# Tile 7's first matrix product: fifteen products per 3x3x2 group, in PSUM chains, in place of seven per 2x2x2 group

## The chip, the cores and the metric

The kernel runs on one core of one Trainium2 chip. The metric is the device time of one execution in microseconds (us), the median of several runs; lower is better. The profile is of one further execution, taken by the hardware profiler.

## The reference

An attention block (RWKV6) is followed by a two-layer block with an exact GELU:

```python
# r, k, v, w: (4, 8, 768, 48), u: (8, 48)
for t in range(S):
    cur = einsum('bhd,bhe->bhde', u * k[t], v[t])
    y[t] = einsum('bhd,bhde->bhe', r[t], state + cur)
    state = w[t][..., None] * state + einsum('bhd,bhe->bhde', k[t], v[t])
x = y.transpose(0, 2, 1, 3).reshape(3072, 384)
h = x @ w_in                       # (384, 2048)
g = 0.5 * h * (1 + erf(h / sqrt(2)))
out = g @ w_out                    # (2048, 384)
```

Everything is float32.

## The kernel before

The 3072 tokens are eight tiles of `T` = 384 tokens. For tile x, `attention(x)` leaves the transposed result in `xT` (three blocks of 128 features by 384 tokens), and `mlp(x)` computes `h` in blocks of 128 columns of `w_in` (16 blocks), the gelu `g` and the output `o`. Both are Python generators. In stage x, a string `PLAN[x]` says in which order they issue: each `.` is the next step of `mlp(x - 1)`, each `s` the next step of `attention(x)`, `f` of `attention(x + 1)`, `l` a load, `x` a sum of parts of `xT` that the next h needs, `w` a step of weight preparation. What the string has not used up is issued at the end of the stage, and after the last stage `mlp(7)` runs alone. Every engine executes its own instructions in the order of issue; waits between engines follow from the data.

In stage 7 the 45 `.` are tile 6's h (27 steps) and its o (18), the 34 `s` the rest of `attention(7)`. Of that, TensorE has the products `kv_ps` (L727), `y_ps` (L768, inside a chunk) and the second part of `y_ps` (L813, from the states); VectorE computes the states `st` from `kv_ps` in a sequential chain (L742) and then reads one column of each `y_ps` (L780, called `fence`). `kv_ps` and `y_ps` come from one pool of two pairs of PSUM banks, so a `y_ps` takes over the banks of a `kv_ps`. ScalarE copies `y_ps` to `xT` (L836, L839), and six small transfers on the SP queue (L843) move the last features of a head to their place.

For tiles 2 to 7, h comes from `h_halves` (L949). Of the three feature blocks, two are taken with the two halves of the weight columns and the two halves of the tokens as a 2x2x2 product by seven products (Winograd's form), the third is multiplied plainly. Per pair of blocks (four pairs `q`) the steps are `first` to `seventh`; every call of `two` issues two matmuls of 192 columns for each factor, by `multiply` (L945). Partial sums go by ScalarE copies (L988, L981, L1008, L1012) and VectorE adds (L999, L1017), the gelu is L977. `h_sums` (L886) has replaced `w_in`'s first feature block in the second half of the columns by a sum with the second, in place, and `sums_of_x` (L907) makes five sums of parts of `xT` (L913). A last part, `rest`, is issued in the middle of the first output product.

`o` comes from `product` (L1082; L1084 is the matmul): eight products of 192 columns each, seven times for two thirds of the tile, and again seven-product forms for the last thirds of two tiles together. `of_g` (L931) makes three sums of parts of `g` for it on VectorE (L937, L939, L941). L1132, L1138, L1141, L1144, L1153, L1181 are VectorE's steps between the output products, `psum()` gives them the banks `mm` (two, shared with `h_ps`).

TensorE issues a float32 product as two instructions, and the counts in the profile are of instructions.

Of the kernel before, what the change touches and what calls it, by code (L numbers as in the profile page):

```python
# [10 lines left out]
F32 = mybir.dt.float32  # L11
# [6 lines left out]
AF = mybir.ActivationFunctionType  # L18
ALU = mybir.AluOpType
PSUM = bass.MemoryType.PSUM  # L20

C = 64
G = 64
D = 48
T = 384
# [7 lines left out]
BANK = 512  # L33
# [28 lines left out]
        "sss.sls.....s......ls.s....s.sssssss..s.....s.ss....s.s.ssss.s.l.ss.l.ls.l...s.l.lslssf.s."  # L62
        ".ffs..lff.xx..xffxffx"
    ),
    7: "......s.s....s.s...s.ssssss...sss.ss...sss..ssss.s...ss...s...s.s.ss.s.s.s.x.x...xxx",
}


def as_float(bits):
# [4 lines left out]
def kernel(  # L74
# [25 lines left out]
    nc = tc.nc  # L100
    NX = rkw.shape[0]
# [4 lines left out]
    NJ = DM // 128  # L106
# [9 lines left out]
    gp = ctx.enter_context(tc.tile_pool(name="gp", bufs=4))  # L116
# [3 lines left out]
    pools = {"d": pairs_of_banks.enter_context(tc.tile_pool(name="pd", bufs=3, space=PSUM))}  # L120
# [3 lines left out]

    def fewer_pairs():
        pairs_of_banks.close()
        pools["d"] = ctx.enter_context(tc.tile_pool(name="pe", bufs=2, space=PSUM))
        pools["u"] = ctx.enter_context(tc.tile_pool(name="pu", bufs=1, space=PSUM))
        for i in range(2):
            u = bank_u(i)  # L130
            nc.tensor.matmul(u, lhsT=zeros[:, 0:128], rhs=zeros, start=True, stop=True)

    def bank_u(i):
        return pools["u"].tile([128, BANK], F32, name="u_ps", tag=f"u{i % 2}")

    def bank(name="o_ps"):
        return ps.tile([128, BANK], F32, name=name, tag="mm", bufs=2)
# [11 lines left out]
    bufs = [io.tile([128, 3 * NP * T], F32, name=f"rkw{i}", bufs=1) for i in range(2)]  # L149
    ALL = NP * T  # L150
# [48 lines left out]
    WI = PIECE // NJ  # L199
    FP = PIECE // DM  # L200
    FI = WI // 128
    w_in_sb = const.tile([128, DF // WI, NJ, WI], F32, name="w_in_sb")
    ins = [(w_in_sb[:, i], w_in.rearrange("(j p) (i c) -> p i j c", p=128, c=WI)[:, i]) for i in range(DF // WI)]
    outs = [(w_out_sb[:, f:f + FP, :], w_out.rearrange("(f p) c -> p f c", p=128)[:, f:f + FP, :]) for f in range(0, NF, FP)]
    pieces = ins + outs
# [50 lines left out]
    for h in masks:  # L256
        if not h:
# [5 lines left out]
                                op0=ALU.logical_shift_right, op1=ALU.logical_shift_left)  # L263
# [4 lines left out]
    a_sb = const.tile([128, 2, NPART * NI, C], F32, name="a_sb")  # L268
# [7 lines left out]
    kx = const.tile([128, 2 * NPART * NI * 3 * C // 2], F32, name="kx")  # L276
# [7 lines left out]
    for i, h in enumerate(QUARTERS[:1]):  # L284
        for a in range(3):
            w_q = (3 - a) * C // 4
            z = q_ints[1 if a == 0 else 2]
            o = i * C if a < 2 else i * C + C // 2
# [18 lines left out]
    def make_quarter_masks():  # L307
        make_fine()
        yield
        for (h, a), m_q in m_qs.items():  # L310
            nc.vector.tensor_tensor(out=quarter[h][a], in0=s_qs[h][:, 0:m_q.shape[1]], in1=m_q, op=ALU.is_equal)
            yield
# [5 lines left out]
    s_home = const.tile([128, DF // 2], F32, name="s_home")  # L318
# [48 lines left out]
    xT_of = {}  # L367
# [480 lines left out]
    FG = 4  # L848
    sums, s3_sb = [], []

    def w_quarter(b, c, k):
        return w_out_sb[:, b * HF + k * FG:b * HF + (k + 1) * FG, c * HM:(c + 1) * HM]

    def w_sums():

        sums.extend(cv.tile([128, HF, HM], F32, name="t", tag="raw", bufs=AHEAD) for _ in range(3))
        for out_, x, y in ((0, (0, 1), (0, 0)), (1, (1, 1), (0, 1)), (0, (1, 1), 0), (2, (1, 0), 0)):
            for k in range(2):
                o = sums[out_][:, k * FG:(k + 1) * FG]
                nc.vector.tensor_sub(o, w_quarter(*x, k), sums[y][:, k * FG:(k + 1) * FG] if isinstance(y, int) else w_quarter(*y, k))  # L860
                yield

    def first_sum():
        for k in range(2):
            nc.vector.tensor_sub(w_quarter(0, 1, k), w_quarter(0, 1, k), w_quarter(0, 0, k))
            yield


    HT = T // 2
    HK = HF // 2  # L870
    s_of, x_sums, s12_of = [], [], {}

    def homes():

        more = [cv.tile([128, PIECE], I64, name="s", tag="raw", bufs=AHEAD).bitcast(F32) for _ in range(2)]
        s3_sb.append(more[0][:, 0:HF * 128].rearrange("p (f c) -> p f c", f=HF))
        x_sums.extend(z[:, i * HT:(i + 1) * HT] for z in (more[0][:, HF * 128:], more[1][:, HF * 128:]) for i in range(2))
        spare = [cv.tile([128, PIECE], F32, name=name) for name in ("f", "f", "e", "e")]
        for i, name in enumerate(("s1", "s2")):
            s12_of[name] = [z[:, 0:FG * 128].rearrange("p (f c) -> p f c", f=FG) for z in spare[2 * i:2 * i + 2]]  # L880
        second = [more[1][:, i * WI:(i + 1) * WI] for i in range(HK)]
        third = [s_home[:, i * WI:(i + 1) * WI] for i in range(HK)]
        fourth = [z[:, FG * 128:] for z in spare]
        s_of.extend((second, third, fourth))

    def h_sums():  # L886

        def w(a, c, k):
            return w_in_sb[:, a * HK + k * 2:a * HK + k * 2 + 2, c, :]

        def pieces_of(i, k):
            return s_of[i - 2][2 * k:2 * k + 2]

        for k in range(2):
            for i in range(2):
                nc.vector.tensor_sub(pieces_of(3, k)[i], w(0, 0, k)[:, i], w(1, 0, k)[:, i])
            yield
            nc.vector.tensor_add(w(1, 0, k), w(1, 0, k), w(1, 1, k))
            yield
            for i in range(2):  # L900
                nc.vector.tensor_sub(pieces_of(2, k)[i], w(1, 0, k)[:, i], w(0, 0, k)[:, i])
            yield
            for i in range(2):
                nc.vector.tensor_sub(pieces_of(4, k)[i], w(0, 1, k)[:, i], pieces_of(2, k)[i])
            yield

    def sums_of_x(x):  # L907

        xT = xT_of[x]
        x00, x01, x10, x11, l0, l1 = (xT[:, c, b * HT:(b + 1) * HT] for c in range(3) for b in range(2))  # L910
        t2, t3, t4, l01 = x_sums
        for o, a, b in ((t3, x11, x01), (x01, x01, x00), (t2, x11, x01), (t4, x10, t2), (l01, l0, l1)):
            nc.vector.tensor_sub(o, a, b)  # L913
            yield

    def mlp(x):
# [3 lines left out]
        xT = xT_of.pop(x)  # L920
        halves = x > 0
        waits, ends = x % 2 == 0, x % 2 == 1
        gs = {}
# [25 lines left out]
        def h_halves():  # L949
# [108 lines left out]
                gelu(q, 1, 1, g_of(q, 1, 1))  # L1058
            late[:] = [rest]

        s1, s2, s3 = [], [], []
        fast = x > 1
        if fast:
            yield from h_halves()
        for n, group in enumerate(() if fast else (0, 2, 1, 3) if halves else range(4)):
            gs[group] = gp.tile([128, FG, T], F32, name="g")
            for f in range(group * FG, (group + 1) * FG):
                h_ps = bank("h_ps")[:, 0:T]
                for j in range(NJ):
                    nc.tensor.matmul(h_ps, lhsT=w_in_sb[:, f // FI, j, f % FI * 128:(f % FI + 1) * 128], rhs=xT[:, j, :],  # L1070
                                     start=(j == 0), stop=(j == NJ - 1))
                t = T - 128 if waits else T
# [31 lines left out]
        def psum():  # L1104
            return bank()[:, 0:HM]
# [6 lines left out]
        if halves:  # L1112
            o_sb = two_rows()
            p1, u2, u3 = (wk.tile([128, HM], F32, name=name, bufs=1) for name in ("p1", "u2", "u3"))
# [27 lines left out]
            for c in range(2):  # L1142
                z = o_sb[1][:, c * HM:(c + 1) * HM]
# [16 lines left out]
        else:  # L1160
            o_ps = [bank()[:, 0:DM] for _ in range(2)]
            for f in range(NF):
                for i, o in enumerate(o_ps):
                    nc.tensor.matmul(o, lhsT=block(i, f // HF, f % HF), rhs=w_out_sb[:, f, :],  # L1164
                                     start=(f == 0), stop=(f == NF - 1))
# [8 lines left out]
        if waits:  # L1174
            _, o2, o1 = psum(), psum(), psum()
# [8 lines left out]
        elif ends:  # L1184
            o_sb = two_rows()
            p1, u2, u3 = p1_alone, *(wk.tile([128, HM], F32, name=name, bufs=1) for name in ("u2", "u3"))
# [14 lines left out]
            for c in range(2):  # L1201
                z = o_sb[1][:, c * HM:(c + 1) * HM]
# [19 lines left out]
    def next_v():  # L1222
        load_v(1, nc.sync)
        yield

    def warm():
        for _ in range(2):
            keep_warm(3, True)
            yield

    def masks_and_sums():
        yield from make_quarter_masks()
        yield from w_sums()
# [3 lines left out]
    for x in range(NX):  # L1237
        if x == 2:
            homes()
        following = attention(x + 1, 0) if x + 1 < NX else iter(())  # L1240
        if x == 0:
            streams = {
                ".": units[0], "s": units[1], "f": following, "c": pieces_of_w, "w": next_v(), "x": warm(),
                "l": chain(weight_in(0, True), islice(second, 5), weight_in(1, True), second, weight_in(2, True)),
            }
        else:
            streams = {
                ".": mlp(x - 1), "s": slots, "f": following,
                "l": load(x + 1, nc.sync),
                "x": sums_of_x(x) if x > 1 else iter(()),  # L1250
                "w": masks_and_sums() if x == 1 else chain(first_sum(), h_sums()) if x == 2 else iter(()),
                "c": pieces_of_w if x == 1 else iter(()),
            }
        for c in PLAN[x]:
            next(streams[c], None)
        for c in ".slxw" if x == 0 else ".slxwc":
            while next(streams[c], streams) is not streams:
                pass
        slots = following
        if x == 1:  # L1260
            fewer_pairs()
    for _ in mlp(NX - 1):
        pass
# [60 lines left out]
```

## Time and profile before

| | us |
|---|---|
| median of 3 runs | 593.41 (592.35 to 593.92) |
| span of the profiled execution, first to last instruction | 595.0 |
| time around that span | none is given |
| TensorE busy, weight loads busy | 576.7, 512.3 |
| VectorE, ScalarE, GpSimdE busy | 440.0, 281.3, 8.0 |
| granted TensorE clock, mean | 0.994 |

In the profile's lines PE is TensorE, PEld its weight loads, DVE VectorE, ACT ScalarE, POOL GpSimdE, SP the queue of DMA issues; `L945` is line 945 of the kernel. A line of the timeline has the start, the length, the engine, the line, the operation, what is written and read, and in brackets how long the engine stood before it and what ended that. The matmuls of L945 start 0.1625 us apart and are shown with 0.326 us each, so they overlap. The profiled execution took 1.6 us more than the median of the runs, so differences are carried over, not times.

### The profile page before, as it was taken

The page shows a single profiled execution, that of the slowest core. Times are in us where ns is not written, and L with a number is a line of the kernel's source. Part 1 is how long each engine was busy: PE and PEld are TensorE (multiplying, and loading weights), DVE is VectorE, ACT ScalarE, POOL GpSimd, SP SyncE. Part 2 cuts the span into 40 slices and gives each one's busy share as a digit, 9 for nine tenths or more (in the row PEclk, how much of TensorE's full clock was granted, in tenths as well). Part 3 has the DMA queues.
Part 4 walks back from the last instruction along what each step waited for, and adds up shares of the span by engine and source line. Part 5 has one row for each costly group of instructions (what it writes and reads, how often), then busy time and mean ns, then how long its engine had stood idle before and what let it go on. Part 6 is the DMA issues. An engine that isn't in the chain of part 4 may idle for free.

```text
span 595.0 us, 17418 instructions
## 1 busy us (share of the span) xinstructions
PE 576.7 (97%) x7536; PEld 512.3 (86%) x7536; DVE 440.0 (74%) x854; ACT 281.3 (47%) x648; POOL 8.0 (1%) x21
## 2 busy tenths in 40 slices
PE   6787999999999999999999999999999999999998
PEld 3574666676699999999999999999999999999997
DVE  6868667888969987687859987688769998421332
ACT  2365889333622358145561458135560465435400
POOL 3100000000000000000000000000000000000000
PEclk8989999999999999999999999999999999999999
DMA  6658571130152211341023310430015200210000
GB/s 235 196 187 296 169 241 57 69 100 1 18 149 77 75 54 22 77 137 36 1 49 93 125 36 16 98 106 15 3 31 162 72 2 5 39 45 0 1 15 33
DMA packets 51004, 46.80 MB, mean 79 GB/s; under 512 B 31728, under 2 KB 36080, under 8 KB 50928
## 3 DMA queue, kind: packets, MB, share of 16 engines
q1 hardware_dynamic: 50832, 45.62, 25.3%
q8 instruction: 59, 0.97, 0.7%
q14 instruction: 17, 0.14, 0.1%
q10 hardware_dynamic: 96, 0.07, 0.0%
HBM read 36.24 MB, written 4.72 MB: 69 GB/s over the span
## 4 chain that ended last, share of the span: by engine, by line
PE 91%; DMA 3%; DVE 3%; issue 1%; ACT 1%; ACTq 0%; SPq 0%; DVEq 0%
PE o_ps L1084 33%; PE h_ps L945 16%; PE u_ps L945 13%; PE h_ps L1070 10%; PE d L604 4%; PE o_ps L1164 4%; PE d L468 2%; PE y_ps L768 2%; PE y_ps L813 2%; PE kv_ps L727 2%; DMA rkw<-in_rkw_dram 1%; DVE st L742 1%; DMA xT<-ysb 1%; DMA raw<-in_w_in_dram 1%; ACT a_sb L529 1%
## 5 line engine op out<-in xcount | busy, mean ns | idle before, releaser
L945 PE MATMUL h_ps<-xT,w_in_sb 128*128 128x192 f32 x480 | 95.4, 330 | 0.0
L945 PEld LDWEIGHTS h_ps<-xT,w_in_sb 128*128 128x128 f32 x480 | 79.8, 190 | 3.4 <-ACT g L977 1.5
L1070 PE MATMUL h_ps<-xT,w_in_sb 128*128 128x384 f32 x192 | 64.5, 491 | 3.0 <-DMA xT<-ysb 2.0
L1070 PEld LDWEIGHTS h_ps<-xT,w_in_sb 128*128 128x128 f32 x192 | 35.7, 190 | 27.6 <-issue 2.6
L1084 PE MATMUL o_ps<-w_out_sb,g 128*128 128x192 f32 x224 | 39.7, 326 | 0.0
L1084 PEld LDWEIGHTS o_ps<-w_out_sb,g 128*128 128x128 f32 x224 | 37.0, 190 | 0.3
L945 PE MATMUL u_ps<-s,w_in_sb 128*128 128x192 f32 x192 | 35.3, 327 | 0.0
L620 ACT COPY a_sb<-d 32x256 f32<-32x256 f32 (+8 forms) x90 | 32.6, 362 | 4.6 <-PE d L604 3.1
L468 PEld LDWEIGHTS d<-rkw 64*64 64x64 f32 x1152 | 19.8, 138 | 15.3 <-issue 10.4
L945 PEld LDWEIGHTS u_ps<-s,w_in_sb 128*128 128x128 f32 x192 | 31.8, 190 | 0.2
L1084 PE MATMUL o_ps<-w_out_sb,f 128*128 128x192 f32 x176 | 31.6, 329 | 0.0
L1084 PE MATMUL o_ps<-t,g 128*128 128x192 f32 x176 | 31.4, 329 | 0.0
L1084 PE MATMUL o_ps<-w_out_sb,e 128*128 128x192 f32 x176 | 31.4, 329 | 0.0
L1084 PE MATMUL o_ps<-t,e 128*128 128x192 f32 x176 | 31.2, 328 | 0.0
L1084 PE MATMUL o_ps<-t,s 128*128 128x192 f32 x176 | 30.9, 327 | 0.0
L742 DVE SCALAR_TENSOR_TENSOR st<-st,tot_sb,kv_ps 128x48 f32<-128x48 f32 x160 | 29.0, 257 | 1.7 <-PE kv_ps L727 1.7
L637 DVE COPY_PREDICATED a_sb<-quarter,d 128x480 f32<-128x480 uint8 (+5 forms) x54 | 23.2, 438 | 8.6 <-PE d L604 7.3
L1084 PEld LDWEIGHTS o_ps<-t,g 128*128 128x128 f32 x176 | 28.7, 190 | 0.4
L1084 PEld LDWEIGHTS o_ps<-w_out_sb,f 128*128 128x128 f32 x176 | 28.7, 190 | 0.3
L1084 PEld LDWEIGHTS o_ps<-w_out_sb,e 128*128 128x128 f32 x176 | 28.7, 190 | 0.3
L1084 PEld LDWEIGHTS o_ps<-t,e 128*128 128x128 f32 x176 | 28.8, 190 | 0.2
L1084 PEld LDWEIGHTS o_ps<-t,s 128*128 128x128 f32 x176 | 28.8, 190 | 0.1
(163 smaller groups left out, 1119.5 us busy)
## 6 DMA issues: line engine op xcount, KB each, us to landing
rkw<-in_rkw_dram SPq DMA_DIRECT2D x54, 256.0 KB, 3.7
raw<-in_w_out_dram SPq DMA_DIRECT2D x8, 768.0 KB, 5.1
v_in<-in_v_dram SPq DMA_DIRECT2D x8, 584.0 KB, 4.0
raw<-in_w_in_dram SPq DMA_DIRECT2D x5, 768.0 KB, 6.9
out_dram<-o_sb SPq DMA_DIRECT2D x20, 192.0 KB, 2.1
rkw<-kx SPq DMA_DIRECT2D x72, 48.0 KB, 2.0
rkw<-in_rkw_dram SPq DMA_DIRECT2D x6, 384.0 KB, 5.9
raw<-in_w_in_dram SPq DMA_DIRECT2D x9, 256.0 KB, 4.9
```

What stands on the lines that cost most here:

```text
L468: nc.tensor.matmul(d[half[p], g, n * width:(n + 1) * width], lhsT=kc[half[g], b, i, p], rhs=right(half[g], b, i, p), start=True, stop=True)
L604: nc.tensor.matmul(o[half[p], i * 3 * C // 2:(i + 1) * 3 * C // 2], lhsT=kc[half[g], n // NI, n % NI, p], rhs=rx[half[g], 2 * n + p], star ...
L620: nc.scalar.copy(out=at[z, g, first:behind, (a + 1) * h:], in_=d[z, :, :, to] if g == slice(None) else d[z, :, to])
L637: nc.vector.copy_predicated(out=an[:, :, :, :, (a + 1) * h:], mask=mask.to_broadcast(data.shape), data=data)
L727: nc.tensor.matmul(kv_ps[half[g], p, i * D:(i + 1) * D], lhsT=k_t(b, i, p, g), rhs=vs(b, i, g)[half[p], 0:D], start=True, stop=True)
L742: nc.vector.scalar_tensor_tensor(out=stq[:, q, c], in0=stq[:, q, c - 1] if c else b4[:, q, NC - 1], scalar=totq[:, q, c:c + 1], in1=kvs[q ...
L768: nc.tensor.matmul(y[p][half[g ^ swap(b)], i * C:(i + 1) * C], lhsT=vs(b, i, g)[half[p]], rhs=at[half[p], g, b * NI + i, :], start=(i == 0 ...
L813: nc.tensor.matmul(ys[b][0][c % 2][half[g ^ swap(b)], i * C:(i + 1) * C], lhsT=src[half[g], o:o + G], rhs=rc[half[g], b, i, c % 2], start= ...
L945: nc.tensor.matmul(o, lhsT=lhsT, rhs=rhs, start=start, stop=True, skip_group_check=True)
L1070: nc.tensor.matmul(h_ps, lhsT=w_in_sb[:, f // FI, j, f % FI * 128:(f % FI + 1) * 128], rhs=xT[:, j, :], start=(j == 0), stop=(j == NJ - 1))
L1084: nc.tensor.matmul(o, lhsT=lhs(j), rhs=rhs(j), start=start and j == 0, stop=(j == HF - 1), skip_group_check=True)
L1164: nc.tensor.matmul(o, lhsT=block(i, f // HF, f % HF), rhs=w_out_sb[:, f, :], start=(f == 0), stop=(f == NF - 1))
```

## The change

For tile 7 alone, h comes from `h_fifteen`. The sixteen blocks of columns are five groups of three (pairs `A`, `B` hold two groups each, `C` one) and one block, number 15, that is left. In each group the 3x3 blocks of weights and the 3x2 blocks of x are multiplied by fifteen products in place of eighteen; block 15 is multiplied plainly, three products over all 384 columns. The order of issue is `ORDER15`. In each group ten products (a, e, f, g, b, c, i, j, k, h) run as a chain: a is copied to SBUF by ScalarE; e to h are added up in one PSUM bank, and after each the partial sum is taken out, by an add, a copy, or a subtraction into another bank, where one of the other five products (p1, p12, p11, p2, p10) is then added; a gelu takes the result. Four banks for this come from the pool of pairs, which is closed (`banks_alone`), two are `u_ps`, two are `mm`.

The weights' sums are made by VectorE in stage 7 (33 steps `w`: one subtraction of 1024 columns that undoes `h_sums` in place, sixteen sums of 512 columns for A and B, sixteen of 128 for C, mostly in place in `w_in_sb`), the ten sums of x in place of five at the stage's end. `PLAN[7]` keeps its `.` and `s` in their order; `w` stand from the 30th `.` on, and the `x` after the 44th, before they stood after the 41st. `of_g` for tile 7 is issued at the end of h, and nothing of h is issued among the output products.

```diff
...
-    7: "......s.s....s.s...s.ssssss...sss.ss...sss..ssss.s...ss...s...s.s.ss.s.s.s.x.x...xxx",
+    7: "......s.s....s.s...s.ssssss...sss.ss...sss..ssss.s...ss.ww.ww.wwsw.ww.ww.ws.s.ss.s.wws.wwwswwww.wwww.wwww.www.xxxx.xxxxxx",
+ORDER15 = (
+    "l0 l1 aA aB aC l2 eA eB eC fA fB fC gA gB gC bA bB bC cA cB cC iA p1A p1B iB p1C iC jA p12A p12B jB p12C jC kA p11A "
+    "p11B kB p11C kC hA p2A p2B hB p2C hC p10A p10B sums p10C"
+)
...
 
     def fewer_pairs():
         pairs_of_banks.close()
-        pools["d"] = ctx.enter_context(tc.tile_pool(name="pe", bufs=2, space=PSUM))
         pools["u"] = ctx.enter_context(tc.tile_pool(name="pu", bufs=1, space=PSUM))
+        pools["stack"] = ctx.enter_context(ExitStack())
+        pools["d"] = pools["stack"].enter_context(tc.tile_pool(name="pe", bufs=2, space=PSUM))
         for i in range(2):
             u = bank_u(i)
             nc.tensor.matmul(u, lhsT=zeros[:, 0:128], rhs=zeros, start=True, stop=True)
+
+    def banks_alone():
+        pools["stack"].close()
+        pool = ctx.enter_context(tc.tile_pool(name="ph", bufs=1, space=PSUM))
+        return [pool.tile([128, BANK], F32, name="c_ps", tag=f"c{i}") for i in range(4)]
...
+    FIRST, THIRD, FIFTH = slice(0, 2), slice(4, 6), slice(2, 4)
+    w15, x15, spare15 = {}, {}, []
+    def w_parts(c, lone):
+        if lone:
+            return [w_in_sb[:, 6, c, 0:128], w_in_sb[:, 6, c, 128:256], w_in_sb[:, 7, c, 0:128]]
+        return [w_in_sb[:, z, c, :] for z in (FIRST, THIRD, FIFTH)]
+    def sums_of_w15():
+        z = w_in_sb[:, HK:, 0, :]
+        nc.vector.tensor_sub(z, z, w_in_sb[:, HK:, 1, :])
+        yield
+        r = bufs[0][:, 0:ALL]
+        pieces = [z.rearrange("p (a c) -> p a c", a=2) for z in
+                  (*(r[:, i * 2 * WI:(i + 1) * 2 * WI] for i in range(3)), *(s_both[i][:, a:a + 2 * WI] for i in range(2) for a in (0, 2 * WI)))]
+        homes_of = {False: pieces[:6], True: [pieces[6][:, i // 2, i % 2 * 128:(i % 2 + 1) * 128] for i in range(4)] + spare15}
+        for lone in (False, True):
+            (w00, w01, w02), (w10, w11, w12), (w20, w21, w22) = (w_parts(c, lone) for c in range(3))
+            e, f, p1, p2, j, b = homes_of[lone]
+            t = w15[lone] = dict(e=e, f=f, p1=p1, p2=p2, j=j, b=b, k=w01, p10=w00, a=w20, i=w22, c=w21, g=w12, h=w10, p11=w11, p12=w02)
+            add, sub = nc.vector.tensor_add, nc.vector.tensor_sub
+            def minus(o, x, y):
+                nc.vector.scalar_tensor_tensor(out=o, in0=x, scalar=-1.0, in1=y, op0=ALU.mult, op1=ALU.subtract)
+            for op, o, x, y in ((add, w20, w10, w20), (add, e, w00, w10), (add, f, e, w12), (sub, b, w01, w21), (add, b, b, w20),
+                                (add, w22, w12, w22), (add, w10, w10, w12), (add, w12, b, w12), (add, w22, w20, w22),
+                                (minus, j, w22, w01), (add, w21, j, w21), (add, p1, f, w02), (sub, w02, w02, w22),
+                                (add, p2, w01, w11), (sub, w11, w11, b), (minus, w10, w10, w01)):
+                op(o, x, y)
+                yield
+    def sums_of_x15(x):
+        xT = xT_of[x]
+        (x00, x01), (x10, x11), (x20, x21) = ([xT[:, c, b * HT:(b + 1) * HT] for b in range(2)] for c in range(3))
+        a, g, b, e, f, j, i, h, k, p10 = (kx[:, i * HT:(i + 1) * HT] for i in range(10))
+        x15.update(a=a, g=g, b=b, e=e, f=f, j=j, i=i, h=h, k=k, p10=p10, p1=x00, p2=x10, c=x20, p12=x01, p11=x11)
+        add, sub = nc.vector.tensor_add, nc.vector.tensor_sub
+        for op, o, y, z in ((add, a, x20, x21), (sub, g, x11, x21), (sub, b, x20, g), (sub, e, x10, b), (sub, f, x00, e),
+                            (add, j, x01, x21), (add, i, x20, j), (add, h, f, g), (add, k, h, j), (add, p10, f, x01)):
+            op(o, y, z)
...
+        def h_fifteen():
+            for group in (0, 2, 1, 3):
+                gs[group] = gp.tile([128, FG, T], F32, name="g")
+            temps = a_sb.rearrange("p g n t -> p (g n t)")
+            blocks = {"A": (0, 8, 4), "B": (2, 10, 6), "C": (12, 13, 14)}
+            ca, cb, cc, cd = banks_alone()
+            x_banks = [bank_u(0), ca, bank_u(1), cb]
+            chain_of = {n: bank("h_ps")[:, 0:2 * HT] for n in "AB"}
+            chain_of["C"] = cc[:, 0:HT]
+            a_lone, o_lone = cc[:, HT:2 * HT], cd[:, 0:T]
+            t_of = {n: temps[:, i * 2 * HT:(i + 1) * 2 * HT] for i, n in enumerate("ABC")}
+            t_of["C"] = t_of["C"][:, 0:HT]
+            x_of, seeds = {}, [0]
+            def region(n, i, j):
+                f = blocks[n][j]
+                z = gs[f // FG][:, f % FG:f % FG + (1 if n == "C" else 2), i * HT:(i + 1) * HT]
+                return z
+            def flat(n, z):
+                return z.rearrange("p (f t) -> p f t", t=HT)
+            def product15(n, o, name, start=False):
+                w = w15[n == "C"][name]
+                for i in range(1 if n == "C" else 2):
+                    lhs = w if n == "C" else w[:, "AB".index(n), i * 128:(i + 1) * 128]
+                    multiply(o[:, i * HT:(i + 1) * HT], lhs, x15[name], start and i == 0)
+            def x_bank(n):
+                o = x_banks[seeds[0] % 4]
+                seeds[0] += 1
+                return o[:, 0:HT if n == "C" else 2 * HT]
+            def step(n, name):
+                o = chain_of[n]
+                if name == "a":
+                    z = a_lone if n == "C" else x_banks[1 + 2 * "AB".index(n)][:, 0:2 * HT]
+                    product15(n, z, "a", True)
+                    nc.scalar.copy(out=t_of[n], in_=z)
+                    return
+                product15(n, o, name, name == "e")
+                z, t = flat(n, o), flat(n, t_of[n])
+                if name in "efg":
+                    nc.vector.tensor_add(region(n, 1, "efg".index(name) * 2 % 3), z, t)
+                elif name == "b":
+                    nc.scalar.copy(out=region(n, 0, 1), in_=z)
+                else:
+                    own, i, j = {"c": ("p1", 0, 2), "i": ("p12", 1, 2), "j": ("p11", 1, 1), "k": ("p2", 0, 1), "h": ("p10", 1, 0)}[name]
+                    if name == "h":
+                        nc.scalar.activation(out=region(n, 0, 0), in_=z, func=AF.Gelu)
+                    x_of[n, own] = o = x_bank(n)
+                    g, o = region(n, i, j), flat(n, o)
+                    if name == "c":
+                        nc.scalar.activation(out=o, in_=z, func=AF.Copy, scale=-1.0)
+                    elif name in "ik":
+                        nc.vector.tensor_sub(o, z, g)
+                    else:
+                        nc.vector.tensor_sub(o, g, z)
+            def own(n, name):
+                o = x_of[n, name]
+                product15(n, o, name)
+                i, j = {"p1": (0, 2), "p12": (1, 2), "p11": (1, 1), "p2": (0, 1), "p10": (1, 0)}[name]
+                nc.scalar.activation(out=region(n, i, j), in_=flat(n, o), func=AF.Gelu)
+            def lone(j):
+                multiply(o_lone, w_in_sb[:, 7, j, 128:256], xT[:, j, :], j == 0)
+                if j == NJ - 1:
+                    nc.scalar.activation(out=gs[3][:, 3, :], in_=o_lone, func=AF.Gelu)
+            for z in ORDER15.split():
+                if z[0] == "l":
+                    lone(int(z[1]))
+                elif z == "sums":
+                    for _ in of_g(0):
+                        pass
+                elif z[0] == "p":
+                    own(z[-1], z[:-1])
+                else:
+                    step(z[1], z[0])
+                yield
+            for _ in of_g(1):
+                pass
         s1, s2, s3 = [], [], []
         fast = x > 1
-        if fast:
+        if x == NX - 1:
+            yield from h_fifteen()
+        elif fast:
             yield from h_halves()
         for n, group in enumerate(() if fast else (0, 2, 1, 3) if halves else range(4)):
             gs[group] = gp.tile([128, FG, T], F32, name="g")
...
-                "x": sums_of_x(x) if x > 1 else iter(()),
-                "w": masks_and_sums() if x == 1 else chain(first_sum(), h_sums()) if x == 2 else iter(()),
+                "x": sums_of_x15(x) if x == NX - 1 else sums_of_x(x) if x > 1 else iter(()),
+                "w": masks_and_sums() if x == 1 else chain(first_sum(), h_sums()) if x == 2 else sums_of_w15() if x == NX - 1 else iter(()),
```

More of the change, by code (lines that the diff above doesn't have):

```diff
@@ L870 @@
     HK = HF // 2
-    s_of, x_sums, s12_of = [], [], {}
+    s_of, x_sums, s12_of, s_both = [], [], {}, []
     def homes():
@@ L880, in homes @@
             s12_of[name] = [z[:, 0:FG * 128].rearrange("p (f c) -> p f c", f=FG) for z in spare[2 * i:2 * i + 2]]
+        s_both.extend((more[1], s_home))
+        spare15.extend(z[:, FG * 128 + i * 128:FG * 128 + (i + 1) * 128] for z in spare[:1] for i in range(2))
         second = [more[1][:, i * WI:(i + 1) * WI] for i in range(HK)]
@@ L1059, in h_halves @@
             late[:] = [rest]
+        def h_fifteen():
[70 more added lines that the diff above has]
+                    step(z[1], z[0])
+                yield
+            for _ in of_g(1):
+                pass
```

## The prediction

> **What bounds the kernel now.** I read the page first (busy shares, then the chain of work that ended last), then that chain in order of time from 500 us on, then the waits, then VectorE's timeline where tile 6 hands over to tile 7.
>
> ```profile
> PE 576.7 (97%) x7536; PEld 512.3 (86%) x7536; DVE 440.0 (74%) x854; ACT 281.3 (47%) x648; POOL 8.0 (1%) x21
> ...
> PE 91%; DMA 3%; DVE 3%; issue 1%; ACT 1%; ACTq 0%; SPq 0%; DVEq 0%
> ```
>
> TensorE is the bound: 91% of the chain. A product that goes shortens the run by its issue time, unless a new wait takes the place. The chain over the last stages:
>
> ```profile
> 520.64 1.56 PE y_ps L768 x96
> 522.20 1.50 PE o_ps L1084 x8
> 523.70 1.56 PE y_ps L813 x96
> 525.25 6.70 PE o_ps L1084 x40
> 531.95 2.77 PE h_ps L945 x16
> ...
> 559.62 1.30 PE o_ps L1084 x8
> 560.92 1.30 PE u_ps L945 x8
> 562.22 29.91 PE o_ps L1084 x184
> ```
>
> Columns: start, length, what. No other engine comes between 500 and 592 us. Tile 7's h is L945, from 531.95 to 562.22 with 1.30 us of output products between: 30.27 - 1.30 = 28.97 us. Two waits lie in it (total us, times, longest):
>
> ```profile
> PEld h_ps L945 <- ACT g L977: 0.2, 1, 0.2
> PEld h_ps L945 <- DVE o_sb L1181: 0.2, 1, 0.2
> ```
>
> VectorE in the handover, and who has ever waited for its state chain (L742; total us, times):
>
> ```profile
> 507.28 0.68 DVE L941 TENSOR_TENSOR s<-g 128x512 f32<-128x512 f32 x1
> 513.80 0.36 DVE L1132 TENSOR_TENSOR u<-o_ps,p 128x192 f32<-128x192 f32 x1 [5.84 <-PE o_ps L1084]
> 514.08 1.28 DVE L1138 TENSOR_TENSOR e<-g,e 128x512 f32<-128x512 f32 x2
> ...
> 516.61 3.24 DVE L742 SCALAR_TENSOR_TENSOR st<-st,tot_sb,kv_ps 128x48 f32<-128x48 f32 x18 [0.26 <-PE kv_ps L727]
> 520.68 0.36 DVE L1141 TENSOR_TENSOR u<-o_ps,p 128x192 f32<-128x192 f32 x1 [0.83 <-PE o_ps L1084]
> ...
> 526.79 0.36 DVE L1153 TENSOR_TENSOR o_sb<-o_ps,u 128x192 f32<-128x192 f32 x1 [4.36 <-PE o_ps L1084]
> 530.31 0.36 DVE L913 TENSOR_TENSOR s<-xT 128x192 f32<-128x192 f32 x1 [3.17 <-DMA xT<-ysb]
> ```
>
> ```profile
>   PE y_ps L768: 0.7, 2
> ```
>
> So VectorE has gaps of 5.8, 4.4 and 3.2 us here, which the change fills; and twice in other stages TensorE stood, 0.7 us together, because y_ps takes the banks of kv_ps and L742 still read them.
>
> **What goes and what comes on TensorE.** One 192-column product is two instructions 0.1625 us apart (16 of L945 from 531.79 to 534.39), 0.325 us. Before: 11 factors x 2 blocks x 4 pairs = 88 products, 28.6 us; the measured 28.97 has 0.37 more, which is the two waits. After: fifteen products on each of five blocks per group of three make 75, 24.4 us; the plain block has 3 products of 384 columns (48 L1070 instructions took 15.6 us in tile 1, so 0.65 us each), 1.95 us. Sum 26.3. Saved: 28.97 - 26.33 = 2.64 us. The two old waits go with their code: the bank behind L1181 is next wanted only by group B's e, 4 us later. The output products stay, except that 1.3 us of h no longer stands between their first eight instructions; their operands are ready (the last gelu of group C ends 0.6 us after h, group 3 is first read 2.6 us after).
>
> **Weight sums on VectorE, beside TensorE until they meet the state chain.** 1 sum of 1024 columns, 16 of 512, 16 of 128. A 512-column sum on w_in_sb took 0.684 us (L898, the same [2, 256] view); in a row, independent sums start every 0.60 us and one that touches what the last one did starts 0.71 after it (L937 to L939, L939 to L941 in the same timeline); 1024 columns, by the slope, 1.14. They may start once L941 is issued, at 507.89, as tile 6's h was last read at 504.4. In the plan's order the large one and ten others precede L1132, one more L1138. By hand: 507.89 + 1.14 + six at 0.60 + four at 0.71 = 515.5 for L1132 (before 513.80); then 0.28 and 0.60, L1138 at 516.35; two of 0.60; the chain L742 at 517.55 (before 515.9). Its operations start every 0.176 us; the 18th, the last on the first y_ps bank, ends at 517.55 + 17 x 0.176 + 0.26 = 520.8. TensorE wants that bank at 520.57 and, as at 535.30 behind L977 (gelu end 535.25, real start about 535.40), starts some 0.15 after the release: **0.35 us stall**. Bounds: 0, as L742 has ended by then today, and 1.5, below. The fences (L780) come after two more sums at about 523.6, and L813 is due at 523.97 by then: free by 0.3, priced at 0. The other five 512 sums and sixteen of 128 (0.2 to 0.3 each) end near 530, while VectorE waits for xT today.
>
> **Ten sums of x instead of five.** 0.28 to 0.38 us each as L913. Two lone products (1.3 us, raw xT) stand ahead, and the first needed sum, a, waits for the last of six xT transfers, 0.6 us after the one that releases L913: about 531.6 against 533.4 wanted. The tenth and the last weight sum end near 535, before the first evacuation. Cost 0, cover 1.7 us; without it each 0.37 us counts. SP's queue gets nothing new.
>
> **Chains in PSUM, the new wait.** Group A's product e must be taken out by an add before f goes on in the same bank: between lie B and C, 0.65 + 0.325 us. By rows: the last matmul ends 0.326 after its start, the add starts 0.04 later and takes 0.558 (L999, 384 columns), the weight load needs 0.05: released 0.974 us after that start; the load would be due at 0.163 + 0.975 - 0.165 = 0.973. An edge. Three such returns (e, f, g) at 0 to 0.1 each: **0 to 0.3, I take 0.1**. VectorE's load in a round of 1.625 us is 0.47 + 0.47 + 0.27. All later returns and seeds have 1.3 us or more; b and c go out by ScalarE in 0.478. Nothing else is queued behind these waits on TensorE but the next group's product, which has its own slack.
>
> A subtraction from PSUM took 0.357 us (L1132), the same size from SBUF 0.354 (L1144). [...]
>
> **Sum:** -2.64 + 0.35 + 0.1 = -2.2 us against the profiled execution: span 595.0, for which no time around it is shown, to 592.8. The median of the runs is 1.6 below that span; moved alike, 593.4 becomes **591.2**. With the stall from 0 to 0.6 and the edges from 0 to 0.3, 590.8 to 591.7. 0.3%, about what a measurement of this kernel can tell from no change, is 1.8 us: 591.6.
>
> **Rival 1: the gaps on VectorE are not that dense (little gained).** If each weight sum starts only when the one before has ended, as the dependent ones do (0.71, and 1.24 for the large): chain start 507.89 + 1.24 + 10 x 0.71 + 0.36 + 0.71 + 1.4 = 518.7, its 18th ends 521.95, stall 1.5. With edges at 0.3: -2.64 + 1.8 = -0.85, **592.6**. For: these sums work in place on one tile, whose views interleave, so waits may be set between sums that share nothing. Against: L941 starts 0.61 after L939, which it does not touch.
> [...]
>
> **Rival 2: slower.** The place is y_ps (L768) behind the state chain; the price is the weight sums at the rate of strided views: L401 takes 2.2 us for 1152 columns, 1.8 ns each, so 512 take 1.06, 0.4 more than counted. Eleven precede the chain: 4.4 us, stall 4.8, -2.64 + 4.8 + 0.1 = +2.2, **595.6**. It decides from a stall of 4.4 on, a mean start distance of about 1.0 us. For: VectorE is queued in order, and nothing gives the chain precedence. Against: L898 measured that very view at 0.684, and rows of 256 are contiguous. What else could hold up the chain by 4 us I do not see, but the plan leaves VectorE no slack there.
>
> That fewer products run than said can be ruled out: 75 and 3 are written out in the order.
>
> **How the numbers follow.** Forecast 0.60, rival 1 0.22 (within 0.3%), rival 2 0.18. The predicted time is the forecast's. The range takes the forecast, a little below it for a stall that vanishes and the spread of the runs (0.5), and rival 1 with a stall of up to 3 us: 590.5 to 594.2. It leaves out rival 2.
>
> **What would show it.** After: 150 instructions of 192 columns and 6 of 384 in tile 7's h; from its first to the first of the last output products some 26.5 us; L768 waiting for L742 by about 0.35 us; no wait of tile 7's first products for xT; no idle time over 0.1 between e, f and g. Wrong if L768 waits over 1 us, if the h stretch is over 27 us, or if L813 waits for a fence.

## The result and the profile after

The changed kernel takes 591.84 us in the median (590.61 to 596.47), the kernel before 593.72 in the runs beside it (592.16 to 596.34), 22 runs each. The ratio is 0.9971 (95% interval 0.9958 to 0.9984): 1.7 us less, between 0.9 and 2.5. That is faster beyond the interval, at the edge of the 0.3% that the prediction drew. It is inside the range.

The profiled executions differ by more, 595.0 against 591.6 us. Of this 1.5 us lie ahead of anything that changed: tile 6's first output matmul starts at 501.83 before and at 500.31 after, and in the seven further profiles below that share the code up to there it starts anywhere from 497.3 to 500.8. So stages are compared by lengths from that matmul on. The page after, by the lines that answer to those of before:

```profile
PE 572.6 (97%) x7502; PEld 509.1 (86%) x7516; DVE 461.9 (78%) x905; ACT 276.6 (47%) x640; POOL 8.0 (1%) x21
...
PE 17%; DVE 4%; issue 0%; DVEq 0%
```

The chain's shares are no longer to be read against those of before: it is followed back only to 465 us, and in the handover it now passes through VectorE. In order of time (start, length, what):

```profile
513.41 0.04 DVE s L955
513.44 0.57 issue
514.02 0.35 DVE u L1278
514.37 0.60 DVE w_in_sb L961
514.96 1.21 DVE e L1284 x2
516.17 3.16 DVE st L754 x18
519.33 0.14 issue
519.47 1.63 PE y_ps L780 x96
521.09 1.50 PE o_ps L1230 x8
522.59 1.77 PE y_ps L825 x96
524.36 6.70 PE o_ps L1230 x40
531.06 3.56 PE c_ps L1004 x16
...
557.52 31.21 PE o_ps L1230 x192
```

L1004, L1230, L780, L825 and L754 are the former L945, L1084, L768, L813 and L742. VectorE has come between TensorE's pieces: weight sums (L955, L961), the add L1278, one more sum, L1284, the state chain, and then y_ps. Its timeline, and who has waited for the chain in the whole run (before: 0.7 us, twice):

```profile
506.36 1.22 DVE L942 TENSOR_TENSOR w_in_sb<-w_in_sb 128x1024 f32<-128x1024 f32 x1
507.50 0.69 DVE L961 TENSOR_TENSOR w_in_sb<-w_in_sb 128x512 f32<-128x512 f32 x1
508.10 0.69 DVE L961 TENSOR_TENSOR rkw<-w_in_sb 128x512 f32<-128x512 f32 x1
508.82 0.69 DVE L961 TENSOR_TENSOR rkw<-rkw,w_in_sb 128x512 f32<-128x512 f32 x1
...
514.02 0.35 DVE L1278 TENSOR_TENSOR u<-o_ps,p 128x192 f32<-128x192 f32 x1
514.28 0.68 DVE L961 TENSOR_TENSOR w_in_sb<-s,w_in_sb 128x512 f32<-128x512 f32 x1
514.88 1.29 DVE L1284 TENSOR_TENSOR e<-g,e 128x512 f32<-128x512 f32 x2
516.09 3.58 DVE L754 SCALAR_TENSOR_TENSOR st<-st,tot_sb,kv_ps 128x48 f32<-128x48 f32 x20
...
530.05 0.63 DVE L972 TENSOR_TENSOR kx<-xT 128x192 f32<-128x192 f32 x2 [0.96 <-DMA xT<-ysb]
```

```profile
  PE y_ps L780: 1.1, 3
```

The gaps of 5.8 and 4.4 us are gone, and one wait has been added to the two there were, of 0.35 us. From the list of waits after 480 us, the two in which TensorE waits for VectorE (total us, times, longest):

```profile
PE y_ps L780 <- DVE st L754: 0.4, 1, 0.4
...
PEld c_ps L1004 <- DVE c_ps L1178: 0.2, 1, 0.2
```

Two stretches sum this up, both from TensorE's timeline: the handover, from tile 6's first output matmul to tile 7's first h matmul, and tile 7's h (before, without the 1.30 us of output products inside it). All later experiments stand in the same table; ratios are to the kernel before, beside it on the same chip. One of E5's ten runs took 1498.17 us and is left out of its ratio.

| kernel | handover, us | h, us | both against before | ratio (95%) |
|---|---|---|---|---|
| before | 29.96 | 28.97 | | |
| after | 30.58 | 26.47 | -1.88 | 0.9971 (0.9958 to 0.9984) |
| E1 sums later | 29.95 | 26.47 | -2.51 | 0.9960 (0.9939 to 0.9982) |
| E2 no sums | 29.95 | 26.47 | -2.51 | 0.9954 (0.9931 to 0.9976) |
| E3 sums alone | 30.75 | 28.97 | +0.79 | 1.0027 (1.0007 to 1.0046) |
| E4 four more | 33.71 | 26.46 | +1.24 | 1.0016 (0.9993 to 1.0040) |
| E5 seed first | 30.51 | 26.33 | -2.09 | 0.9981 (0.9960 to 1.0001) |
| E6 C apart | 30.80 | 27.08 | -1.05 | 0.9984 (0.9964 to 1.0005) |
| E1 and E5 | 29.96 | 26.32 | -2.65 | 0.9935 (0.9909 to 0.9960) |
| E7 after, shifted | 30.37 | 26.47 | -2.09 | one run |
| E8 E1, shifted | 29.95 | 26.47 | -2.51 | one run |

The change takes 2.50 us out of h and gives 0.62 back in the handover. The experiments ask where these 0.62 come from, and what the 0.14 us are by which h is longer than its 26.33 us of issue (75 products at 0.325 us and three at 0.65). The intervals of the ratios are 0.3 to 0.5% wide, so what is said of single terms rests on the stretches.

### The profile page after: what moved, and what is told of

The parts are those of the page before. It is cut to its first block, busy times and chain, and to the rows that moved or that the text cites. A ratio compares the mean times of both kernels' runs of the same rounds, so it can differ in the third digit from the quotient of the medians.

```text
span 591.6 us, 17427 instructions
## 1 busy us (share of the span) xinstructions
PE 572.6 (97%) x7502; PEld 509.1 (86%) x7516; DVE 461.9 (78%) x905; ACT 276.6 (47%) x640; POOL 8.0 (1%) x21
## 5 line engine op out<-in xcount | busy, mean ns | idle before, releaser
L1004 PE MATMUL h_ps<-xT,w_in_sb 128*128 128x192 f32 x408 | 81.2, 330 | 0.1
L1004 PEld LDWEIGHTS h_ps<-xT,w_in_sb 128*128 128x128 f32 x408 | 67.7, 190 | 3.1 <-ACT g L1036 1.2
L1216 PEld LDWEIGHTS h_ps<-xT,w_in_sb 128*128 128x128 f32 x192 | 35.8, 190 | 24.6 <-ACT kx L429 0.8
L1230 PE MATMUL o_ps<-w_out_sb,g 128*128 128x192 f32 x224 | 39.5, 326 | 0.0
L1230 PEld LDWEIGHTS o_ps<-w_out_sb,g 128*128 128x128 f32 x224 | 37.0, 190 | 0.3
L1230 PE MATMUL o_ps<-w_out_sb,f 128*128 128x192 f32 x176 | 31.6, 329 | 0.0
L1230 PE MATMUL o_ps<-w_out_sb,e 128*128 128x192 f32 x176 | 31.4, 329 | 0.0
L1230 PE MATMUL o_ps<-t,g 128*128 128x192 f32 x176 | 31.4, 329 | 0.0
L1230 PE MATMUL o_ps<-t,e 128*128 128x192 f32 x176 | 31.2, 328 | 0.0
L1230 PE MATMUL o_ps<-t,s 128*128 128x192 f32 x176 | 30.9, 327 | 0.0
L754 DVE SCALAR_TENSOR_TENSOR st<-st,tot_sb,kv_ps 128x48 f32<-128x48 f32 x160 | 28.9, 258 | 0.9 <-PE kv_ps L739 0.8
L1004 PE MATMUL u_ps<-s,w_in_sb 128*128 128x192 f32 x160 | 29.5, 327 | 0.0
L1230 PEld LDWEIGHTS o_ps<-t,g 128*128 128x128 f32 x176 | 28.7, 190 | 0.4
L1230 PEld LDWEIGHTS o_ps<-w_out_sb,e 128*128 128x128 f32 x176 | 28.7, 190 | 0.3
L1230 PEld LDWEIGHTS o_ps<-w_out_sb,f 128*128 128x128 f32 x176 | 28.7, 190 | 0.3
L1230 PEld LDWEIGHTS o_ps<-t,e 128*128 128x128 f32 x176 | 28.8, 190 | 0.2
L480 PE MATMUL d<-rkw 64*64 64x64 f32 (+1 forms) x1152 | 22.6, 229 | 6.6 <-DMA rkw<-in_rkw_dram 3.2
L1230 PEld LDWEIGHTS o_ps<-t,s 128*128 128x128 f32 x176 | 28.9, 190 | 0.1
```

Of the source, the lines that this page charges most:

```text
L480: nc.tensor.matmul(d[half[p], g, n * width:(n + 1) * width], lhsT=kc[half[g], b, i, p], rhs=right(half[g], b, i, p), start=True, stop=True)
L754: nc.vector.scalar_tensor_tensor(out=stq[:, q, c], in0=stq[:, q, c - 1] if c else b4[:, q, NC - 1], scalar=totq[:, q, c:c + 1], in1=kvs[q ...
L1004: nc.tensor.matmul(o, lhsT=lhsT, rhs=rhs, start=start, stop=True, skip_group_check=True)
L1230: nc.tensor.matmul(o, lhsT=lhs(j), rhs=rhs(j), start=start and j == 0, stop=(j == HF - 1), skip_group_check=True)
```

## The experiments

**E1, the sums later.** Four 512-column sums move behind the fences, by the plan alone (an excerpt of `PLAN[7]`, from the 30th to the 41st step of the product stream):

```diff
- .30 w w .31 w w .32 w w s w .33 w w .34 w w .35 w s .36 s .37 s s .38 s .39 w w s .40 w w w s w w w w .41
+ .30 w w .31 w w .32 w w s w .33 w w .34 w   .35   s .36 s .37 s s .38 s .39     s .40 w w w w s w w w w .41
```

(`.30` is tile 6's 30th step; behind .41 the 128-column sums follow in their order.)

> The after kernel with two of the eleven 512-column weight sums that precede the state chain, and two that precede the fences, moved behind the fences; the order of everything else is kept. Theory (the handover got longer because VectorE's queue has weight sums ahead of the state chain, so y_ps waits for its banks): the wait of y_ps for the state chain goes from 0.35 us to 0, and the stretch from tile 6's first output matmul to tile 7's first h matmul from 30.58 to 30.0 to 30.2 us (29.96 before the change; the upper end if the 0.21 us inside the second y_ps products has another cause). Total 0.4 to 0.6 us less than after. Rival (something else in the new stage, such as the weight sums taking turns with TensorE's reads, costs it): the stretch stays at 30.5 or more.

TensorE's timeline in the handover:

```profile
518.92 1.63 PE L780 MATMUL y_ps<-a_sb,v_in 64*64 64x64 f32 x96
520.48 1.57 PE L1230 MATMUL o_ps<-w_out_sb,e 128*128 128x192 f32 x8
521.98 1.63 PE L825 MATMUL y_ps<-rkw,st 64*64 64x64 f32 x96
```

In the after kernel the last of these was

```profile
522.52 1.84 PE L825 MATMUL y_ps<-rkw,st 64*64 64x64 f32 x96
```

No bracket stands behind L780 in E1: the wait is gone, and with it 0.21 us inside L825 (called the pause below). The handover is back at 29.95. Here 512-column sums run during L825 too (three start from 522.03 to 523.36 us), so that VectorE reads and writes beside TensorE is not what lengthens it. The theory holds, the rival falls.

**E2, no sums.** `op(o, x, y)` in `sums_of_w15` is left out, so that tile 7 is multiplied by old data.

> The after kernel without the 32 weight sums of 512 and 128 columns (the undoing of the in-place sum stays); their results are not computed, so the products of tile 7 multiply old data. Theory: the whole 0.62 us that the handover gained is theirs, the stretch comes to 29.9 to 30.1 us, h stays at 26.5, the total is 0.6 us below after. Rival (the 0.21 us inside the second y_ps products belong to something else): 30.2.

29.95 us as well: what the sums cost is all of the 0.62, and E1 gets all of it back by order alone.

**E3, the sums alone**, in the kernel before (shown against the after kernel; the plan issues five sums of x, as before):

```diff
-        if x == NX - 1:
-            yield from h_fifteen()
-        elif fast:
+        if fast:
...
-                "x": sums_of_x15(x) if x == NX - 1 else sums_of_x(x) if x > 1 else iter(()),
+                "x": sums_of_x(x) if x > 1 else iter(()),
```

> The kernel before with the weight sums of the change alone: same places in the plan, tile 7's h by seven products as before (it multiplies weights that the sums have altered), five sums of x. Theory: the handover costs the same as in the after kernel, 30.4 to 30.6 us in place of 29.96, h stays at about 29.0, the total is 0.4 to 0.6 us above before. Rival (the sums of x or the new banks cost it): no more than 30.1.

The handover is 30.75, a little above what I gave: y_ps waits the same 0.35 us, and the pause inside L825 is 0.38 instead of 0.21. h stays at 28.97. By the ratio the sums alone make the kernel slower, beyond its interval.

**E4, four more sums** ahead of the state chain:

```diff
                 op(o, x, y)
+                if o is f and not lone:
+                    for _ in range(4):
+                        op(o, x, y)
                 yield
```

> The after kernel with one 512-column weight sum done five times in place of once (the same result again), ahead of the state chain. Theory (nothing gives the state chain precedence, and VectorE is full there): each repetition moves y_ps by its 0.6 to 0.72 us, in all 2.4 to 2.9 us: stretch 33.0 to 33.5 us, total 2.4 to 2.9 above after, which makes it slower than the kernel before by 0.5 to 1.0. Rival (there is slack on VectorE that takes it in): under 1 us.

```profile
522.81 1.63 PE L780 MATMUL y_ps<-a_sb,v_in 64*64 64x64 f32 x96 [2.18 <-DVE st L754]
```

y_ps starts 2.90 us later than in the after kernel, counted from the first output matmul: 0.72 for each repetition, which is the distance of two dependent sums (508.10 and 508.82 in the after kernel). Part of it is not at y_ps: an output product waits 0.8 us for its add, the former L1132, which stands behind the sums too. The handover of 33.71 us is above the 33.0 to 33.5 I gave, since the pause inside L825 is 0.42 here. By the stretches the kernel is 1.24 us slower than before; the ratio's interval holds 1. There is no slack at this place: by the stretches, some 2 us of extra work on VectorE undo the change.

**E5, the seed first.** In the chain step h, the subtraction that fills p10's bank before p10 is added there (the seed) is issued before the gelu, which reads the same chain bank:

```diff
-                    if name == "h":
-                        nc.scalar.activation(out=region(n, 0, 0), in_=z, func=AF.Gelu)
...
                         nc.vector.tensor_sub(o, g, z)
+                    if name == "h":
+                        nc.scalar.activation(out=region(n, 0, 0), in_=z, func=AF.Gelu)
```

> The after kernel with the two readers of chain product h in the other order: VectorE's subtraction, which seeds the bank for p10, before ScalarE's gelu of the same bank. Theory (the two reads of a bank are taken one after the other, so the seed waited for the gelu, 0.49 us, and p10B for the seed): the 0.15 us over the issue time of tile 7's h shrinks, from 26.47 to 26.33 to 26.40 us; the gelu is later but nothing waits for it. Rival (the 0.1 us at p10B has another cause): 26.45 or more.

In the after kernel VectorE's seed of group B (L1178) and TensorE's p10 of B, from two timelines:

```profile
555.67 0.56 DVE L1178 TENSOR_TENSOR c_ps<-g,h_ps 128x384 f32<-128x384 f32 x1 [1.39 <-ACT g L1170]
```

```profile
556.28 0.92 PE L1004 MATMUL c_ps<-kx,w_in_sb 128*128 128x192 f32 x4
```

Four matmuls take 0.81 us when nothing holds them, here 0.92. With the seed first (both engines' timeline; the subtraction is L1176 here, the gelu L1178):

```profile
555.48 0.56 DVE L1176 TENSOR_TENSOR c_ps<-g,h_ps 128x384 f32<-128x384 f32 x1 [1.39 <-ACT g L1184]
556.08 0.49 ACT L1178 ACTIVATE g<-h_ps 128x384 f32<-128x384 f32 x1 [0.69 <-DVE c_ps L1176]
```

Now the gelu waits for the seed, as the bracket says; before, the seed waited for the gelu. The bracket of the seed here names another gelu, which ended at 555.38 us, but its own product ended then too (555.37), and earlier seeds start as long after their products (0.10 to 0.12 us). Why the two go one after the other is not separated: both read the bank `h_ps`, and the gelu also writes into the tile `g` between the columns that the seed reads. h comes to 26.33 us, its issue time exactly. The total of this kernel is not to be told from that of after, nor, by its interval, from that of before.

**E6, C apart.** In the order of issue, e and f of C no longer stand between A and B, and C's next steps move back with them (an excerpt of `ORDER15`):

```diff
- eA eB eC fA fB fC gA gB gC bA bB bC cA cB cC iA p1A p1B iB p1C iC jA p12A p12B
+ eA eB fA fB gA gB eC bA bB fC cA cB gC iA p1A bC p1B iB cC p12A p1C iC jA p12B
```

> The after kernel with the order of tile 7's products changed: group C's e and f no longer stand between A and B's e, f and g, so that each chain returns after 0.65 us in place of 0.975. Theory (the evacuation by an add takes 0.97 us from the last matmul's start and has no slack): the two returns that lose C wait 0.33 to 0.45 us each, h goes from 26.47 to 27.1 to 27.4 us. Rival (the returns had slack, or waits between chains are hidden): h under 26.7.

```profile
PEld h_ps L1004 <- DVE g L1164: 0.7, 2, 0.4
```

Two returns wait, the two that were named, and h is 0.61 us longer, 0.3 each: just under what I gave. With 0.325 us less between, 0.30 more are waited for, so the returns of the after kernel have some 0.02 us to spare.

**E1 and E5 together.**

> The sums later and the seed first together. Theory: both add up, 0.5 to 0.75 us less than after, 2.4 to 2.6 us less than the kernel before, stretch 30.0 to 30.2 and h 26.33 to 26.40 us. Rival (one of them only moves a wait): no more than the better of the two.

They add up: 29.96 and 26.32 us, 2.65 below before, and the lowest ratio of all, 0.9935; its median over seven runs was 590.25 us against 593.74. Measured it is 3.9 us (2.4 to 5.4), to which the 2.65 of the stretches belong at the lower end. No wait is left in the handover or in h except the 0.2 us at the change to 64-row products, which were there before.

**E7 and E8, the pause.** The 0.21 us inside L825 is no wait that the trace names. In E4 and E6 it lies behind the 33rd of the 96 matmuls, in the others at the same place, some 0.6 us after L825's start; all five kernels above with a late y_ps have it (0.14 to 0.43 us), and none of the others. E7 is the after kernel and E8 is E1, and both get eight zero products at the start of stage 7:

```diff
+        if x == NX - 1:
+            keep_warm(8)
         for c in PLAN[x]:
```

> The after kernel with eight extra zero products (16 TensorE instructions) at the start of stage 7, long before the handover. It is about the 0.2 us pause inside the second y_ps products, which in every kernel with a late y_ps lies behind the 33rd or 34th of their 96 matmuls. Theory A (the pause is at a border of the instruction stream): it moves 8 matmuls forward, to about the 25th. Theory B (it hangs on the data, one state or one wait): it stays behind the 33rd. If there is no pause at all, it depends on something that neither names.

> The kernel with the sums later (no late y_ps, no pause) with the same eight extra products. Theory A and B alike: no pause; the second y_ps products take 1.55 us. If a pause shows up, the late y_ps is not what makes it, and the border of the stream alone is.

TensorE in E7:

```profile
520.57 1.63 PE L780 MATMUL y_ps<-a_sb,v_in 64*64 64x64 f32 x96 [0.35 <-DVE st L754]
522.12 1.57 PE L1230 MATMUL o_ps<-w_out_sb,e 128*128 128x192 f32 x8
523.62 1.63 PE L825 MATMUL y_ps<-rkw,st 64*64 64x64 f32 x96
```

y_ps waits its 0.35 us, but L825 has no pause; in E8 it has none either (1.63 us). So a late y_ps alone does not bring the pause, and that it is not behind the 33rd matmul speaks against theory B. It did not move to the 25th matmul either, as theory A had it. But each of the two is a single profile, on another chip than E1 to E6 and with no unshifted kernel profiled beside it, so that the shift made the pause vanish is not shown. (By their one run each, 594.32 and 594.13 us, both are slower than the 592.63 of the kernel before beside them; with runs of one kernel up to 5.6 us apart, from 591.30 to 596.94 for the kernel before beside E1, single runs do not tell such differences.)

The traces offer one candidate that no run tests. The page has a DMA queue of instructions, q8 (0.97 MB in 59 transfers, so about 16 KB each). Its last transfer ahead of L825 starts 1.45 us (E6), 1.91 (E4), 2.02 (E3), 2.10 (after) and 2.20 us (E5) before L825 in the kernels with the pause, and 2.13 (E7) to 3.09 us (E1) before it in the others. The pause is longer where the transfer is later, but E7 at 2.13 and E1 and E5 together at 2.20 have none, so this is a hint and no more. What the pause is stays open.

The wait by itself costs 0.41 us of TensorE's time: 30.37 - 29.96 in E7, and the same is left in after, E3, E5 and E6 when their pauses are taken off.

## Why the prediction was right, and where not

**The products.** Saved 2.64 forecast, 2.50 measured. The count and both durations held; the two old waits went. E5 shows the issue time of 26.33 to the hundredth.

**The weight sums.** The forecast stall of 0.35 us is the bracket of the after kernel, 0.35; it costs 0.41 of TensorE's time (E7 and the others without their pauses), 0.06 more, which nothing here explains. The hand-counted starts held: from the large sum to L1278 7.7 us (506.36 to 514.02; forecast 7.6, from 507.89 to 515.5), to the state chain 9.7 (forecast 9.66). E1 and E4 show the cause, E3 that it needs nothing else of the change.

**Left out: the pause inside L825**, 0.21 us, which the sum has no term for. It is the largest miss, and its cause is not settled.

**The chains.** The edge was sized right, 0.973 against 0.974, and taken at 0.1; the returns of e, f and g cost 0.02 at most. The step that failed is "all later returns and seeds have 1.3 us or more": that counted the add from the end of its product, and not that ScalarE's gelu of the same bank goes first (E5). It cost 0.14, so the term came out near its size for a wrong reason.

**The sums of x, the fences, the output:** priced at 0, and the first sum starts at 530.05, 0.84 us before tile 7's first matmul, the fences end 0.4 before L825. The cover held.

**The sum** was -2.2, the stretches give -1.88, the runs -1.7 (0.9 to 2.5): a right mechanism, 0.3 too much, most of it the pause. The forecast range of the likeliest case, 590.8 to 591.7, was missed by a tenth.

**The rivals.** Rival 1 asked for weight sums that each wait for the one before. They do not: the second 512-column sum starts 0.60 after the first (508.10, 507.50), though both work on `w_in_sb`; the third, which reads what the second wrote, starts 0.72 after it. The rival falls. Rival 2 asked for the rate of strided views. It falls with 0.68 to 0.69 us for each 512-column sum, but its place was right: E4 puts 2.9 us there, and by the stretches the gain is gone.

The prediction's rows of 192 columns differ by 0.003 us between a source in PSUM and SBUF alone (0.357 and 0.354). The adds of 384 columns show no more: L1164 with a source in PSUM took 0.557 us (six of them), L999 before from SBUF 0.558 (the four in tile 7).

## What to carry to other kernels

Where one engine is the bound, count the products that go in its issue time (2.64 us counted here, 2.50 measured), and then look for the queue that pays for them: here VectorE's, in which 9.7 us of preparatory sums and adds stood ahead of a chain that releases a bank. At one place of the order such sums cost the handover nothing (29.95 us in E1, 29.96 before), at another, a few steps away, each further one cost 0.72 us (E4), so place them by what is queued behind them. When you price an evacuation, look for other work on the same bank and the same result tile: here a gelu on another engine went first, and changing the order of the two was worth 0.14 us (E5, h from 26.47 to 26.33).

## What the runs showed of the hardware

In five of the six profiles with a late y_ps, a dense stretch of 64x64 products paused for 0.14 to 0.43 us without a wait for another engine in the trace, behind the 33rd of its 96 matmuls in E4 and E6 and some 0.6 us after its start in the others; in the five profiles with y_ps on time none did. And what lies ahead of tile 6's output differed by 4.5 us (497.3 to 501.8) between profiles with the same code up to there, more than twice what the change brings: stretches of the trace told apart what totals could not.
